# Two layers of an MLP behind attention on one core: the seven-product frames' half-units at 4, 2, 4, 4, one sum for two, and the conversion of w_out paced at two steps a pair

## The chip, the core and the metric

The kernel runs on one core of a Trainium2 chip. The metric is the device time in microseconds (us), the median of several runs. The engines are TensorE (PE, matrix products), VectorE (DVE), ScalarE (ACT), GpSimd (POOL) and SyncE (SP), which here only issues DMAs.

## What is computed

Attention over 4 batches, 8 heads, 576 tokens and 64 columns a head (half of the heads see the last 32 tokens, half see every 32nd), its output as 2304 tokens x 512, and then two MLPs of the same form:

```
def _moe_ref(x, w_in, w_out):        # x 2304x512, w_in 512x2048, w_out 2048x512
    h = x @ w_in
    r = np.maximum(h, 0.0)
    return (r * r) @ w_out           # called twice, with weights of its own each time
```

All is float32 to the caller. The kernel splits each operand of an MLP into a high part (fp32r) and the remainder, and takes three products: high x high, high x low, low x high.

## The kernel before

First attention and the first layer run mixed; then the first layer runs alone, beside the conversion of the second layer's weights, up to about 512 us; then comes one narrow block of 256 tokens of layer 2 (to about 545 us), and from there on the frames.

*Layer 1.* A list `steps` of pairs (block, f) is walked in order: mm1 of the next step (products into ps_h, then on ACT r, sq and gh, the high part of the squared relu, and on DVE gl, the remainder), then mm2 of this one (products of gh and gl into the four ps_y). After a block's last step ACT evicts ps_y (L1085) and the tile o is stored in y_dram (L1087): in the last two blocks from ACT's own queue, else from SP. Each step has 8 points (`point`), and at each a credit grows by PACES, 0.6 for w_out and 0.68 for w_in; a whole credit lets `conv2_by` issue one unit of converting layer 2's weights. A pair of w_out quarters is nine units: exponent and sign on raw and others (L263 on ACT), the high part of each quarter (L368, ACT), its remainder (rest2, DVE), the sums of quarters for the seven products (sums_1 to sums_3), and their high part (L420, ACT). Both quarters of a pair are stored in w_mem by one DMA of 1 MB (L378), the sums by another (L426); both tiles are used again by the next pair.

*The narrow block.* Eight steps; the products with w_out are at L1142. The last step's 12 stand inside the first frame.

*The frames.* Blocks of 512 tokens use a scheme of seven products for eight (as Strassen's). A frame works on one pair of hidden tiles: it makes the products with w_in of the next pair, in four visits (L1274), and puts the seven products with w_out of the current pair between them, as 14 half-units of three matmuls (L1301). All of a frame's visits write one PSUM tile of 512 columns, ps_m (in the first frame visits 3 and 4 have another). Visit 1 (12 matmuls) is copied away by ACT (u, L1354); visit 2 (6) overwrites the left half and is added to c11 by DVE (L1109); visit 3 (12) writes both halves, which DVE reads in three sums, u3, a22 and u4; visit 4 (12) writes both halves again, and DVE makes c from them (128x512). Behind each visit stands a gap with 3, 3, 5 and 3 half-units. Each engine runs its instructions in the order in which the code issues them. There are 31 frames with half-units, and the first one, with the 12 products of the narrow block in threes.

```
gaps = todo[:3], todo[3:6], todo[6:11], todo[11:]       # seven()
visit(k, q, ps, ("11", 0), ("s2", 1)); ... each(gaps[0])
visit(k, q, ps, ("12", 2)); add(c11, ps[:, :HT], c11); ... each(gaps[1])
visit(k, q, ps, ("s1", 3), ("s3", 4)); ... each(gaps[2])       # behind it the three sums
visit(k, q, ps, ("s4", 5), ("22", 6)); add(of["c"], ps, u); ... each(gaps[3])
```

Of the kernel before, what the change touches and what calls it, by code (L numbers as in the profile page):

```python
# [17 lines left out]
P = 128  # L18
# [6 lines left out]
NF = DFF // P  # L25
# [34 lines left out]
AT_V, AT_XN = P + 2 * P + 126, P + 2 * P + 126 + 5 * 260  # L60
OTHERS = AT_XN + 256 + 64

PACES = 0.6, 0.68
N_WARM = 8
ZEROS = (0, 0, 0, 0, 0, 2, 2, 2, 2, 4, 4, 4)

# [98 lines left out]
def r32(ap):  # L165
    return ap.bitcast(F32)
# [3 lines left out]
def tile_attention_then_two_mlps(  # L170
# [9 lines left out]
    nc = tc.nc  # L180
# [191 lines left out]
    def rest2(i):  # L372
        v = val[half1 + i].rearrange("p (h m) -> p h m", h=2)
        w = w_nat[i]
        nc.vector.tensor_tensor(out=w[:, :, 1], in0=v, in1=r32(w[:, :, 0]), op=ALU.subtract)
        done2.add(i)
        if i < NF and i % 2:
            nc.sync.dma_start(out=w_mem[i // 2][:, :4 * U], in_=r32(xall[:, units_at:units_at + 4 * U]))  # L378

    s_sum = {}  # L380

# [661 lines left out]
    def mm2(s, point):  # L1043

        k, f = steps[s]
        layer, j = blocks[k]
        t0, n = BLOCKS[layer][j]
        ne = tiles_of(k)
        ws = [ready(("out", layer, f + e)) for e in range(ne)]
        h, lo = gh.pop(s), gl.pop(s)  # L1050

        if f == 0:
            ys[k] = [ps_y.tile([P, 512], F32, tag=f"y{c}", name="ps_y") for c in range(KC)]
        end = f + ne == NF

        def narrow_at(s):
            return s < len(steps) and tiles_of(steps[s][0]) > 1

        todo = []
        for c, y in enumerate(ys[k]):  # L1060
            cols = slice(c * P, (c + 1) * P)
            for i, (a, gp) in enumerate(((0, h), (1, h), (0, lo))):
                for e, w in enumerate(ws):
                    g0 = e * n
                    todo.append((i, c, y[:, :n], w[:, a, cols], gp[:, g0:g0 + n]))
        if not end:

            todo.sort(key=lambda t: t[0] == 2)
        places = [-(-len(todo) * (i + 1) // 4) - 1 for i in range(3)]
        last = {t[1]: m for m, t in enumerate(todo)}  # L1070
        seen = set()
        for m, (i, c, y, lhsT, rhs) in enumerate(todo):
            product(
                y,
                lhsT=lhsT,
                rhs=rhs,
                start=f == 0 and c not in seen,
                stop=end and m == last[c],
                halves=m == len(todo) - 1 and rhs.shape[-1] == TB and narrow_at(s + 2),
            )  # L1080
            seen.add(c)
            one_small()
            if end and m == last[c]:
                t = tile_of("s" if c % 2 and j >= NB - 2 else "pt")[:, :n]
                nc.scalar.activation(out=t, in_=y, func=AF.Copy, scale=W_BACK)  # L1085
                queue = nc.scalar if j >= NB - 2 else nc.sync
                queue.dma_start(out=y_dram[:, c, t0:t0 + n], in_=t)  # L1087
            if m in places:
                point()

# [10 lines left out]
    def rest(hi, lo, src):  # L1101
        tt(lo, src, r32(hi), ALU.subtract)
# [5 lines left out]
    def add(dst, src, to, sign=1.0):  # L1108
        nc.vector.scalar_tensor_tensor(  # L1109
            out=dst, in0=src, scalar=sign * W_BACK, in1=to, op0=ALU.mult, op1=ALU.add  # L1110
        )
# [45 lines left out]
    def narrow(s, point):  # L1157
        q = steps[s][1] // 2
        ring_load(q)
        narrow_w(q + 1)  # L1160
        work = x_work.setdefault(NB + 1, x_works(NB + 1))
        if q + 1 < NF // 2:
            if q == 0:
                load_x(NB + 1, 0)
                load_x(NB + 1, 1)
            elif q > 1:
                all_of(work[q - 2])
            mm1(s + 1, point)
            point()
            for m, one in enumerate(narrow_products(s)):  # L1170
                one()
                if m % 3 == 2:
                    point()
            return
        while n_conv2[0] < len(conv2):
            conv2_by(1)
        all_of(work[-1])
        todo = narrow_products(s)
        frame([todo[3 * i:3 * i + 3] for i in range(4)], (NB + 1, 0), False)
        t0, n = BLOCKS[1][0]  # L1180
        for c, y in enumerate(ys[NB]):
            t = tile_of("pt")
            nc.scalar.activation(out=t, in_=y, func=AF.Copy, scale=W_BACK)
            nc.sync.dma_start(out=out[t0 + c * P:t0 + (c + 1) * P, :], in_=t)
# [128 lines left out]
    def frame(gaps, nxt, cur, copies=((), (), ()), end=False, x=((), (), ()), late=()):  # L1313

        k, q = nxt
        if not of:
            of["r"] = gpool.tile([P, TB], F32, tag="r", name="r", bufs=1)
            of["c"] = gpool.tile([P, TB], F32, tag="sq", name="c", bufs=1)
            shapes = {"bh": ("qk0", 4), "bl": ("qk1", 4), "ah": ("qk2", 3)}
            for t, (tag, n) in shapes.items():  # L1320
                of[t] = fpool.tile([P, n * HALF], F32R, tag=tag, name=t, bufs=1).rearrange(
                    "p (i n) -> p i n", i=n)
            for t, n in (("al", 2), ("al2", 1)):
                of[t] = gpool.tile([P, 3 * HALF], F32R, tag="gl", name=t, bufs=2)[
                    :, 48:48 + n * HALF].rearrange("p (i n) -> p i n", i=n)
        r, c = (of[t].rearrange("p (h n) -> p h n", h=2) for t in ("r", "c"))
        a11, a22, a21, a12 = r[:, 0], r[:, 1], c[:, 0], c[:, 1]
        ah, al, bh, bl = (of[t] for t in ("ah", "al", "bh", "bl"))
        sums_x, high_x, rest_x = x

        def positive(t, src):
            nc.scalar.activation(out=t, in_=src, func=AF.Relu)
            nc.scalar.activation(out=t, in_=t, func=AF.Square)

        if cur:
            s13, s24 = (
                gpool.tile([P, TB + P], F32, tag="gh", name="s", bufs=2)[:, :TB].rearrange(
                    "p (i n) -> p i n", i=2)
                for _ in range(2)
            )  # L1340
            high(ah[:, 2], a12)
            tt(s13[:, 0], a21, a22, ALU.add)
            tt(s13[:, 1], a11, a21, ALU.subtract)
            rest(ah[:, 2], of["al2"][:, 0], a12)
            tt(s24[:, 0], s13[:, 0], a11, ALU.subtract)
            tt(s24[:, 1], a12, s24[:, 0], ALU.subtract)
        each(copies[0])
        ps = ps_h.tile([P, TB], F32, tag="h", name="ps_m")
        visit(k, q, ps, ("11", 0), ("s2", 1))
        m, u = (vpool.tile([P, 512], F32, tag="val", name="u") for _ in range(2))  # L1350

        c11, u2 = m[:, :HT], m[:, HT:]
        u4, u3 = u[:, :HT], u[:, HT:]
        nc.scalar.activation(out=m, in_=ps, func=AF.Copy, scale=W_BACK)  # L1354
        tt(u2, c11, u2, ALU.add)
        each(copies[1])
        if cur:
            high(ah[:, 0:2], s13)
            high(bh[:, 2:4], s24)
        each(copies[2])  # L1360
        each(gaps[0])
        if end:
            first_sum()
        visit(k, q, ps, ("12", 2))
        add(c11, ps[:, :HT], c11)
        if cur:
            rest(bh[:, 2:4], bl[:, 2:4], s24)
            rest(ah[:, 0:2], al, s13)
        each(sums_x)
        if end:  # L1370
            each(high_x)
            each(rest_x)
        positive(a11, c11)
        high(bh[:, 0], a11)
        if not end:
            each(high_x)
        each(gaps[1])
        if nxt == pairs7[0]:
            ps = ps_a.tile([P, TB], F32, tag="a", name="ps_m")
        visit(k, q, ps, ("s1", 3), ("s3", 4))  # L1380
        add(u3, ps[:, HT:], u2)
        add(a22, ps[:, :HT], u3)
        add(u4, ps[:, :HT], u2)
        positive(a22, a22)
        high(bh[:, 1], a22)
        rest(bh[:, 0], bl[:, 0], a11)
        if not end:
            each(rest_x)
        each(gaps[2])
        each(late)  # L1390
        rest(bh[:, 1], bl[:, 1], a22)
        visit(k, q, ps, ("s4", 5), ("22", 6))
        add(of["c"], ps, u)
        squares(of["c"])
        each(gaps[3])
# [4 lines left out]
    def first_sum():  # L1400
        acc["p1"] = tile_of("pt")
        nc.scalar.activation(out=acc["p1"], in_=banks["11"], func=AF.Copy, scale=W_BACK)
# [105 lines left out]
    def seven():  # L1508
        copies, sums = None, []
        for n, (k, q) in enumerate(pairs7[:-1]):  # L1510
            todo = [one for name in ORDER for one in n_unit(k, q, name)]
            gaps = todo[:3], todo[3:6], todo[6:11], todo[11:]
            end = q == NF // 2 - 1 or n + 2 == len(pairs7)
            more = k < last7
            x = [[], [], []]
# [131 lines left out]
```

## Time and profile before

| | |
|---|---|
| median of 3 runs | 867.05 us (866.18 to 868.54) |
| the profiled execution | 866.58 us |
| its span, from the first to the last instruction | 864.8 us |
| mean granted clock of TensorE, share of the higher level | 0.999 |
| busy: PE / DVE / ACT | 851.5 / 683.0 / 526.1 us |
| DMA over the span | 155.21 MB, 179 GB/s |

A matmul is pipelined: its row begins when it starts, and its end is modelled, so that two neighbours overlap in the rows. How fast TensorE works is read from the distance between starts. An idle time in brackets counts from the modelled end of the row before.

### The profile page before, as it was taken

What the parts mean: (1) busy time and instruction counts of PE and PEld (TensorE: products, weight loads), DVE (VectorE), ACT (ScalarE), POOL (GpSimd) and SP (SyncE); (2) the same over time, 40 slices, a digit from 0 to 9 for tenths busy, and PEclk for the clock granted to TensorE, in tenths of its full rate; (3) what the DMA queues carried; (4) which work ended last, traced back from release to release, by engine and by line L of the source; (5) the groups of instructions that cost most, each with busy time, mean ns of one, the idle gap of its engine ahead of it and who ended that gap; (6) DMA issues with size and microseconds to landing.
All of it is one profiled execution on the core that took longest, in us unless ns stands there. A gap on an engine that the chain in (4) does not pass through costs nothing. (4 is left out here: it accounts for less than half of the span.)

```text
span 864.8 us, 16060 instructions
## 1 busy us (share of the span) xinstructions
PE 851.5 (98%) x5719; PEld 771.6 (89%) x5719; DVE 683.0 (79%) x1742; ACT 526.1 (61%) x1216; POOL 17.7 (2%) x15
## 2 busy tenths in 40 slices
PE   9899999999999999999999999999999999999997
PEld 8778888888788888899788899899999999999997
DVE  5899895489776777477889977678888889888877
ACT  6987775467665665375767774555554564556442
POOL 0610000000000000000000000000000000000000
PEclk9999999999999999999999999999999999999999
DMA  8965721222222221167988486376668667766764
GB/s 257 343 216 154 240 65 43 89 78 73 72 82 97 75 61 53 70 219 293 338 324 265 146 281 232 131 221 207 195 186 281 193 187 240 245 188 194 231 186 130
DMA packets 81247, 155.21 MB, mean 179 GB/s; under 512 B 7440, under 2 KB 36240, under 8 KB 78096
## 3 DMA queue, kind: packets, MB, share of 16 engines
q1 hardware_dynamic: 80016, 152.62, 54.2%
q10 hardware_dynamic: 1152, 1.57, 0.5%
q8 instruction: 45, 0.74, 0.3%
q14 instruction: 34, 0.28, 0.1%
HBM read 127.95 MB, written 26.21 MB: 178 GB/s over the span
## 5 line engine op out<-in xcount | busy, mean ns | idle before, releaser
L971 PE MATMUL ps_h<-xall,w 128*128 128x512 f32 (+1 forms) x1153 | 247.3, 358 | 0.0
L971 PEld LDWEIGHTS ps_h<-xall,w 128*128 128x128 f32 x1153 | 185.1, 188 | 25.9
L971 PE MATMUL ps_y<-gh,w 128*128 128x512 f32 (+1 forms) x640 | 156.8, 375 | 2.3 <-ACT gh L1020 1.6
L971 PEld LDWEIGHTS ps_y<-gh,w 128*128 128x128 f32 x640 | 107.7, 188 | 20.5 <-ACT gh L1020 2.2
L1274 PE MATMUL ps_m<-xall,s 128*128 128x256 f32 x768 | 104.8, 279 | 0.6 <-DVE u L1109 0.6
L1274 PEld LDWEIGHTS ps_m<-xall,s 128*128 128x128 f32 x768 | 95.5, 188 | 1.8 <-DVE u L1109 1.0
L1301 PE MATMUL ps_y<-w,bh 128*128 128x256 f32 x496 | 91.8, 278 | 0.0
L1014 ACT ACTIVATE r<-ps_h 128x512 f32<-128x512 f32 x80 | 47.4, 593 | 62.1 <-PE ps_h L971 52.8
L971 PE MATMUL ps_y<-gl,w 128*128 128x512 f32 (+1 forms) x324 | 83.9, 370 | 0.5 <-DVE gl L1025 0.5
L1274 PE MATMUL ps_m<-xall,w 128*128 128x256 f32 x576 | 83.4, 281 | 0.0
L1301 PEld LDWEIGHTS ps_y<-w,bh 128*128 128x128 f32 x496 | 75.3, 188 | 0.0
L1274 PEld LDWEIGHTS ps_m<-xall,w 128*128 128x128 f32 x576 | 74.3, 188 | 0.4 <-ACT u L1354 0.4
L1301 PE MATMUL ps_y<-w,ah 128*128 128x256 f32 x372 | 70.0, 278 | 0.0
L1025 DVE TENSOR_TENSOR gl<-sq,gh 128x512 fp32r<-128x512 f32 x80 | 55.2, 690 | 17.6 <-ACT gh L1020 13.2
L1301 PE MATMUL ps_y<-w,bl 128*128 128x256 f32 x248 | 68.8, 277 | 0.0
L1023 DVE TENSOR_TENSOR sq<-r 128x512 f32<-128x512 f32 x38 | 26.3, 692 | 49.2 <-ACT r L1014 49.2
L971 PEld LDWEIGHTS ps_y<-gl,w 128*128 128x128 f32 x324 | 55.7, 188 | 10.4 <-DVE gl L1025 1.2
L1109 DVE SCALAR_TENSOR_TENSOR u<-ps_m,u 128x256 f32<-128x256 f32 x96 | 40.4, 421 | 26.4 <-PE ps_m L1274 26.3
L1099 ACT ACTIVATE ah<-c 128x256 fp32r<-128x256 f32 x33 | 13.7, 418 | 71.3 <-DVE c L1283 71.1
L1301 PEld LDWEIGHTS ps_y<-w,ah 128*128 128x128 f32 x372 | 56.7, 189 | 0.0
L676 ACT ACTIVATE s<-s,m 96x128 f32<-96x128 f32 (+2 forms) x88 | 34.3, 390 | 34.3 <-DVE m L560 33.7
L1301 PE MATMUL ps_y<-w,al 128*128 128x256 f32 x186 | 51.6, 277 | 0.0
(121 smaller groups left out, 1505.7 us busy)
## 6 DMA issues: line engine op xcount, KB each, us to landing
w<-w_mem SPq DMA_DIRECT2D x221, 256.0 KB, 2.8
raw<-moe_w_in_d SPq DMA_DIRECT2D x32, 512.0 KB, 6.1
w_mem<-xall SPq DMA_DIRECT2D x16, 1024.0 KB, 5.3
raw<-moe_w_out_d SPq DMA_DIRECT2D x24, 512.0 KB, 5.1
xall<-w_mem SPq DMA_DIRECT2D x8, 1024.0 KB, 5.1
qk<-loc_qk_d SPq DMA_DIRECT2D x12, 416.0 KB, 3.1
out_d<-o SPq DMA_DIRECT2D x17, 256.0 KB, 2.6
others<-moe_w_out_d SPq DMA_DIRECT2D x8, 512.0 KB, 7.1
```

The lines of the kernel that those rows point to most:

```text
L676: nc.scalar.activation(out=blk, in_=blk, func=AF.Exp, scale=-1.0, bias=m[:nq, j:j + 1], accum_out=dens[i][:nq, j:j + 1],)
L971: nc.tensor.matmul(y[:, c:c + w], lhsT=lhsT, rhs=rhs[:, c:c + w], start=start and c == 0, stop=stop and c + w == n,)
L1014: nc.scalar.activation(out=r, in_=ps, func=AF.Relu, scale=W_BACK)
L1023: nc.vector.tensor_tensor(out=sq, in0=r, in1=r, op=ALU.mult)
L1025: nc.vector.tensor_tensor(out=lo, in0=sq, in1=r32(h), op=ALU.subtract)
L1099: nc.scalar.activation(out=hi, in_=src, func=AF.Copy)
L1109: nc.vector.scalar_tensor_tensor(out=dst, in0=src, scalar=sign * W_BACK, in1=to, op0=ALU.mult, op1=ALU.add)
L1274: nc.tensor.matmul(ps[:, half * HT:(half + 1) * HT], lhsT=w[:, j * P:(j + 1) * P], rhs=x[:, j], start=half == 0 and j == 0 and m == 0, sto ...
L1301: nc.tensor.matmul(banks[name][:, t * HALF:(t + 1) * HALF], lhsT=g[:, rows], rhs=w, start=first and t == 0 and m == 0, stop=end and t == 1 ...
```

## The change

Five edits. (1) `gaps` holds 4, 2, 4 and 4 half-units; in the first frame the 12 products of the narrow block stand 4, 2, 4 and 2. (2) u3 and u4, two additions of u2 to the halves of visit 3's tile, become one instruction of 512 columns, ahead of a22. (3) PACES for w_out is 0.56. (4) Each quarter of w_out is stored by itself as soon as its remainder is made, in two DMAs of 512 KB. (5) The stores of y_dram of the last two blocks go from SP as the others do; and in the frame that ends a block the remainder of ah stands ahead of visit 2 and its sum instead of behind.

```diff
-PACES = 0.6, 0.68
+PACES = 0.56, 0.68
...
-        if i < NF and i % 2:
-            nc.sync.dma_start(out=w_mem[i // 2][:, :4 * U], in_=r32(xall[:, units_at:units_at + 4 * U]))
+        if i < NF:
+            a = i % 2 * 2 * U
+            nc.sync.dma_start(
+                out=w_mem[i // 2][:, a:a + 2 * U],
+                in_=r32(xall[:, units_at + a:units_at + a + 2 * U]),
+            )
...
-                queue = nc.scalar if j >= NB - 2 else nc.sync
-                queue.dma_start(out=y_dram[:, c, t0:t0 + n], in_=t)
+                nc.sync.dma_start(out=y_dram[:, c, t0:t0 + n], in_=t)
...
-        frame([todo[3 * i:3 * i + 3] for i in range(4)], (NB + 1, 0), False)
+        frame((todo[:4], todo[4:6], todo[6:10], todo[10:]), (NB + 1, 0), False)
...
         if end:
             first_sum()
+            rest(ah[:, 0:2], al, s13)
         visit(k, q, ps, ("12", 2))
         add(c11, ps[:, :HT], c11)
         if cur:
             rest(bh[:, 2:4], bl[:, 2:4], s24)
+        if cur and not end:
             rest(ah[:, 0:2], al, s13)
...
-        add(u3, ps[:, HT:], u2)
+        add(
+            u.rearrange("p (h n) -> p h n", h=2),
+            ps.rearrange("p (h n) -> p h n", h=2),
+            u2.unsqueeze(1).to_broadcast([P, 2, HT]),
+        )
         add(a22, ps[:, :HT], u3)
-        add(u4, ps[:, :HT], u2)
...
-            gaps = todo[:3], todo[3:6], todo[6:11], todo[11:]
+            gaps = todo[:4], todo[4:6], todo[6:10], todo[10:]
```

TensorE from the second half-unit behind visit 1 to visit 3 of a frame, before. Visits are L1274, half-units L1301; bh, bl, ah and al are parts of the squared relu (a number behind al tells two of them apart).

```order
L1301 MATMUL ps_y<-w,bh 128x256 x2
L1301 MATMUL ps_y<-w,bl 128x256
L1301 MATMUL ps_y<-w,ah 128x256 x2
L1301 MATMUL ps_y<-w,al_5986 128x256
L1274 MATMUL ps_m<-xall,w 128x256 x6
L1301 MATMUL ps_y<-w,ah 128x256 x2
L1301 MATMUL ps_y<-w,al_5986 128x256
L1301 MATMUL ps_y<-w,bh 128x256 x2
L1301 MATMUL ps_y<-w,bl 128x256
L1301 MATMUL ps_y<-w,bh 128x256 x2
L1301 MATMUL ps_y<-w,bl 128x256
L1274 MATMUL ps_m<-xall,s 128x256 x12
```

The same place after (the lines are three further on):

```order
L1304 MATMUL ps_y<-w,bh 128x256 x2
L1304 MATMUL ps_y<-w,bl 128x256
L1304 MATMUL ps_y<-w,ah 128x256 x2
L1304 MATMUL ps_y<-w,al_5994 128x256
L1304 MATMUL ps_y<-w,ah 128x256 x2
L1304 MATMUL ps_y<-w,al_5994 128x256
L1277 MATMUL ps_m<-xall,w 128x256 x6
L1304 MATMUL ps_y<-w,bh 128x256 x2
L1304 MATMUL ps_y<-w,bl 128x256
L1304 MATMUL ps_y<-w,bh 128x256 x2
L1304 MATMUL ps_y<-w,bl 128x256
L1277 MATMUL ps_m<-xall,s 128x256 x12
```

One half-unit (two matmuls and one) has moved from behind visit 2 to in front of it; visit 3 begins three matmuls sooner behind visit 2.

DVE in the same frame, before, from visit 2's sum (the first row) to c:

```order
L1109 SCALAR_TENSOR_TENSOR u<-ps_m,u 128x256
L386 TENSOR_TENSOR bl<-s,bh 128x512
L386 TENSOR_TENSOR al<-s,ah 128x512
L1109 SCALAR_TENSOR_TENSOR u<-ps_m,u 128x256
L1109 SCALAR_TENSOR_TENSOR r<-ps_m,u 128x256
L1109 SCALAR_TENSOR_TENSOR u<-ps_m,u 128x256
L386 TENSOR_TENSOR bl<-r,bh 128x256 x2
L1109 SCALAR_TENSOR_TENSOR c<-ps_m,u 128x512
```

And after:

```order
L1112 SCALAR_TENSOR_TENSOR u<-ps_m,u 128x256
L390 TENSOR_TENSOR bl<-s,bh 128x512
L390 TENSOR_TENSOR al<-s,ah 128x512
L1112 SCALAR_TENSOR_TENSOR u<-ps_m,u 128x512
L1112 SCALAR_TENSOR_TENSOR r<-ps_m,u 128x256
L390 TENSOR_TENSOR bl<-r,bh 128x256 x2
L1112 SCALAR_TENSOR_TENSOR c<-ps_m,u 128x512
```

The sum of 512 columns stands where the first of 256 stood, and the last of the three is gone.

ACT at the end of the fourth layer-1 block, before: r, sq and gh belong to a step, o to the evictions, the rest to the conversion.

```order
L368 ACTIVATE xall<-val 128x2x256
L1014 ACTIVATE r<-ps_h 128x512
L1019 ACTIVATE sq<-r 128x512
L1020 ACTIVATE gh<-sq 128x512
L1085 ACTIVATE o<-ps_y 128x256
L1087 DMA y_dram<-o 128x256
L368 ACTIVATE xall<-val 128x2x256
L1085 ACTIVATE o<-ps_y 128x256
L1087 DMA y_dram<-o 128x256
L1085 ACTIVATE o<-ps_y 128x256
L1087 DMA y_dram<-o 128x256
L1085 ACTIVATE o<-ps_y 128x256
```

And after, from a step's r to the next conversion:

```order
L1018 ACTIVATE r<-ps_h 128x512
L1023 ACTIVATE sq<-r 128x512
L1024 ACTIVATE gh<-sq 128x512
L1089 ACTIVATE o<-ps_y 128x256 x4
L368 ACTIVATE xall<-val 128x2x256 x2
L1018 ACTIVATE r<-ps_h 128x512
L1023 ACTIVATE sq<-r 128x512
L1024 ACTIVATE gh<-sq 128x512
L424 ACTIVATE xall<-raw 128x4x256
```

The four evictions stand together, without the issues of their stores, and both L368 copies of a pair follow them.

## Rows read from the trace of the kernel before

**Rows 1.** the page, busy us (share of the span) and instructions of each engine
```profile
PE 851.5 (98%) x5719; PEld 771.6 (89%) x5719; DVE 683.0 (79%) x1742; ACT 526.1 (61%) x1216; POOL 17.7 (2%) x15
```

**Rows 2.** windows by stage: length, then busy PE, PEld, DVE, ACT, POOL; PEclk, DMA
```profile
366.00:422.00 56.00, 53.90 (x419) 50.59 (x419) 41.54 (x75) 35.79 (x60) 0.00 (x0) 1.00 0.72 262
512.00:545.00 33.00, 32.70 (x216) 29.67 (x215) 24.64 (x42) 18.39 (x31) 0.00 (x0) 1.00 0.68 241
...
553.00:854.00 301.00, 300.99 (x2594) 300.32 (x2594) 253.41 (x552) 160.68 (x347) 0.00 (x0) 1.00 0.67 210
```

**Rows 3.** timeline of TensorE, one frame: start, us, engine, line, operation, count [idle <-releaser]
```profile
561.86 0.85 PE L1274 MATMUL ps_m<-xall,w 128*128 128x256 f32 x6
...
564.25 0.87 PE L1274 MATMUL ps_m<-xall,w 128*128 128x256 f32 x6
...
566.02 1.54 PE L1274 MATMUL ps_m<-xall,s 128*128 128x256 f32 x12
...
569.10 0.87 PE L1274 MATMUL ps_m<-xall,s 128*128 128x256 f32 x6
...
571.58 0.40 PE L1274 MATMUL ps_m<-xall,w 128*128 128x256 f32 x2
```

**Rows 4.** timeline of DVE in the same frame
```profile
565.16 0.43 DVE L1109 SCALAR_TENSOR_TENSOR u<-ps_m,u 128x256 f32<-128x256 f32 x1 [0.48 <-PE ps_m L1274]
...
567.60 0.42 DVE L1109 SCALAR_TENSOR_TENSOR u<-ps_m,u 128x256 f32<-128x256 f32 x1 [0.81 <-PE ps_m L1274]
...
568.40 0.41 DVE L1109 SCALAR_TENSOR_TENSOR u<-ps_m,u 128x256 f32<-128x256 f32 x1
...
570.72 0.69 DVE L1109 SCALAR_TENSOR_TENSOR c<-ps_m,u 128x512 f32<-128x512 f32 x1 [0.43 <-PE ps_m L1274]
```

**Rows 5.** timeline of TensorE, end of a layer-1 block
```profile
407.78 2.90 PE L971 MATMUL ps_h<-xall,w 128*128 128x512 f32 x13
411.60 0.74 PE L971 MATMUL ps_y<-gh,w 128*128 128x256 f32 x4 [0.91 <-ACT gh L1020]
...
413.22 0.62 PE L971 MATMUL ps_y<-gh,w 128*128 128x256 f32 x4
...
415.27 2.90 PE L971 MATMUL ps_h<-xall,w 128*128 128x512 f32 x12
418.01 0.62 PE L971 MATMUL ps_y<-gh,w 128*128 128x512 f32 x2
...
421.32 0.86 PE L971 MATMUL ps_y<-gl,w 128*128 128x512 f32 x3
```

**Rows 6.** timeline of ACT there; ACTq is its queue of DMA issues
```profile
408.12 1.06 ACT L420 ACTIVATE xall<-others 128x1024 fp32r<-128x1024 f32 x1 [2.36 <-DMA w_mem<-xall]
...
417.82 0.34 ACTq L1087 DMA_DIRECT2D y_dram<-o  x1
```

**Rows 7.** timeline of TensorE, narrow block's start and the first frame
```profile
511.31 1.10 PE L971 MATMUL ps_h<-xall,w 128*128 128x256 f32 x8
512.71 2.11 PE L1142 MATMUL ps_y<-xall,gh 128*128 128x512 f32 x8 [0.30 <-ACT gh L1020]
514.66 0.96 PE L1142 MATMUL ps_y<-xall,gl 128*128 128x512 f32 x4
...
544.70 0.84 PE L1142 MATMUL ps_y<-xall,gh 128*128 128x512 f32 x3
...
547.04 1.58 PE L1274 MATMUL ps_m<-xall,s 128*128 128x256 f32 x12
548.46 0.61 PE L1142 MATMUL ps_y<-xall,gh 128*128 128x512 f32 x2
548.91 0.39 PE L1142 MATMUL ps_y<-xall,gl 128*128 128x512 f32 x1
549.93 0.97 PE L1274 MATMUL ps_m<-xall,s 128*128 128x256 f32 x6 [0.63 <-DVE u L1109]
```

**Rows 8.** the page, DMA issues: KB each, us from issue to landing
```profile
w_mem<-xall SPq DMA_DIRECT2D x16, 1024.0 KB, 5.3
```

More of the change, by code (lines that the diff above doesn't have):

```diff
@@ L1352, in frame @@
         c11, u2 = m[:, :HT], m[:, HT:]
-        u4, u3 = u[:, :HT], u[:, HT:]
+        u3 = u[:, HT:]
         nc.scalar.activation(out=m, in_=ps, func=AF.Copy, scale=W_BACK)
```

## Prediction

> **What bounds the kernel now.** First the page: TensorE (PE) is busy 98% of a span of 864.8 us [rows 1]. A change can therefore gain in two ways only: where PE stands still, or where its matmuls start closer together. Next the busy times by stage, where the granted clock is 1.00, the higher of TensorE's two levels (2.4 GHz), in every one [rows 2]. From 553 to 854 us, the second layer's seven-product frames, PE is busy 300.99 of 301.00 us: nothing is missing there, DVE's 253 us fit beside it, and whatever is removed from DVE or ACT is worth nothing until PE itself moves. From 366 to 422 us PE is busy 53.90 of 56.00 us: there it waits. Third, TensorE's rows in time order. A row's start is a fact and its end is modelled, so I count from start to start.
>
> **One frame.** The frame of [rows 3] starts its visits at 561.86, 564.25, 566.02 and 569.10 us and the next frame at 571.58: 9.72 us. Its 84 matmuls are all 256 columns wide, but the spacing has two values: 21 matmuls in 2.39 us (0.1138 each), 15 in 1.77 (0.118), 27 in 3.08 (0.114), 21 in 2.48 (0.118). I call 0.1138 fast and 0.1182 slow. The spacing changes at each step from half-units to a visit. Had all 84 been fast, the frame would last 9.56 us, so the slow part costs 0.16. The order of the frame shows what stands between two such steps: 21, 15, 27, 21 matmuls, all odd. After the change it is 24, 12, 24, 24, all even.
>
> All visits of a frame write one PSUM tile, so each also waits until what the last one left there is read. From [rows 3] and [rows 4] I take two distances. A visit's last matmul begins one spacing ahead of the next row, for the second visit 564.25 + 5 x 0.118 = 564.84; DVE's read begins at 565.16, that is 0.32 later. The tightest visit of the frame, at 571.58, comes 0.17 after the read it waits for (570.72 + 0.69 = 571.41). So a visit can begin no sooner than last matmul + 0.32 + DVE's work + 0.17. After the third visit DVE's work is three sums, from 567.60 to 568.81; 0.17 more gives 568.98, and the visit came at 569.10: 0.12 to spare.
>
> **The change, part by part.**
>
> *Gaps 4, 2, 4, 4 and the joint sum, 31 frames.* PE's instructions are the same in number. Behind visit 1 a half-unit more (3 matmuls, 0.34 us) can only relax visit 2, which ACT's copy u releases and which does not wait now. Behind visit 2 there are 6 matmuls in place of 9. With the last matmul at L, the third visit would come at L + 7 x 0.1138 = L + 0.80; the limit is L + 0.32 + 0.43 + 0.17 = L + 0.92. It waits 0.12. Behind visit 3, 12 in place of 15: nominal L + 13 x 0.1138 = L + 1.48; DVE now does one 128x512 sum and one 128x256 sum in place of three of 256. An addition of 512 from PSUM lasts 0.69 in this frame (the c row), one of 256 0.41 to 0.43 [rows 4], so L + 0.32 + 0.69 + 0.03 + 0.42 + 0.17 = L + 1.63, a wait of 0.15. The removed addition thus gives DVE 0.07 us back where the gap was cut by 0.34, which uses up the 0.12 to spare. Behind visit 4, 12 in place of 9: the next frame gains 0.34 over a margin that is now nil.
>
> What the two waits cost depends on the spacing between them. Fast everywhere, the frame is 53 spacings of 0.1138 (6.03) + 0.92 + 1.25 + 1.63 = 9.83 us, where 1.25 is the third visit's 11 spacings up to its last matmul: +0.11 a frame, +3.4 over 31. With the two values taking turns as now it is 9.95: +0.23, +7.1 in all. Slow everywhere, 10.10: +0.38, +11.8. Fast everywhere with no wait, 9.56: -0.16, -5.0. These are the ends; I take +3.4. My reason is the oddness above: layer 1's steps hold 24 products, an even count, and run at one spacing (12 of 512 columns from 415.27 to 418.01 [rows 5] are 0.228 each, twice 0.114), while the stretches that change pace are the odd ones. It is a pattern in rows, not a known cause.
>
> On the spacing the Trainium skill has a rule, in "TensorE: Matmul & The Clock Gate", Part 1, section "Wait — 56ns, not 53.3ns?": at full clock start-to-start is N / 2.4 GHz plus about 2.5 ns whatever comes before, so by that page an estimate of 109 ns for 256 columns. The trace disagrees on the value (113.8 and 118) and shows two of them. By that rule the order of visits and half-units is worth nothing and only waits count; this is the first rival below.
>
> *w_out conversions at 0.56 a point.* Nine units make a pair of w_out quarters and a step has 8 points, so a pair now takes 9 / 0.56 = 16 points, two whole steps; before it took 15 and its place wandered against the steps. I put three stalls of PE down to this. (A) ACT waits 2.36 us for a store of w_mem to release its tile, up to 408.12 [rows 6], its relu and gh come late, and PE waits for gh: from 407.78 to 413.22 it takes 5.44 us for 12 products of 512 columns (2.74; the last is in two pieces) and 6 of 256 (0.68): 2.0 us [rows 5]. (B) At the end of a block ACT's four evictions o stand between conversions and four issues of stores on ACT's own queue, 0.34 each [rows 6]; 8 products starting at 418.01 take 3.31 us where 8 x 0.228 = 1.82 are due: 1.5 us [rows 5]. (C) From 511.31 to 514.66, 8 products of 256 and 8 of 512 take 3.35 where 0.91 + 1.82 are due, with a wait for gh between: 0.6 us [rows 7]. After the change the order has r, sq and gh ahead of the conversions' copies in each step, and the four evictions in a row: I take A, B and C as gone, 4.1 us. If what they wait for only moves, they stay: 0.
>
> *Store in two halves.* Eight 1 MB stores become sixteen of 512 KB; the first half no longer waits for the second quarter. A 1 MB store lands in 5.3 us at the median [rows 8]. In a pair's 10.9 us (two steps) even two full landings back to back would end in time, which is why I take this as no cost; it is costed together with A above.
> The Trainium skill speaks against it, in "DMA: Bandwidth & Descriptors", section "Bandwidth": transfers should be batched to 1 MiB or more. By that page's single-transfer fit (2 us plus the bytes at 436 GB/s) two halves are an estimate of 6.4 us in all against 4.4 for one; no run here shows a 512 KB store to w_mem yet, the rows have 5.3 for the 1 MB one.
>
> *Eight y stores from ACT to SP.* ACT loses eight issues, in B 4 x 0.34 = 1.4 us of its time. On SP they wait for ACT's evictions, and the next loads of weights stand behind them; those are loaded several us ahead of use, so nothing on PE is late by the 1.5 us over which four evictions last (four times about 0.4, an addition of that width on DVE being 0.42).
>
> *The first frame* (545 to 553 us), whose half-units are 512 wide: 4, 2, 4, 2. Visit 2 there waits for ACT's copy: from 544.70 to 547.04 six products and the visit take 2.34 where 6 x 0.228 + 6 x 0.116 = 2.06 are due, 0.28; visit 4 waits for DVE's sums, the product at 548.91 taking 1.02 for 0.23, 0.8 [rows 7]. One product of 0.228 more ahead of each removes the first and leaves 0.5 to 0.6 of the second: -0.5. Visit 3 has a tile of its own and doesn't wait.
>
> *The earlier rest in the four block ends* puts 0.69 of DVE ahead of the addition that visit 3 waits for. With 6 matmuls of cover gone this may cost up to 0.5 in four frames; DVE does it while visit 2 runs, so I take 0, with +2 as the other end.
>
> *Conversions end one step later* (8 pairs, 1 point each), which puts them into the narrow stage, where DVE is busy 24.64 of 33.00 us [rows 2]: covered but for +0.2, a small reserve with no row of its own.
>
> Sum: -2.0 - 1.5 - 0.6 - 0.5 + 0.2 = -4.4, and +3.4 from the frames: -1.0. The profiled execution took 866.58 us (span 864.8 and 1.8 around it); 865.6 is 866.05 on the median, which lies 0.47 above it.
>
> **The rivals.**
> 1. *The spacing keeps taking turns* whatever the count. For it: nothing but parity speaks of why it turns. Then the frames cost 7.1: 866.58 - 4.4 + 7.1 + 0.47 = 869.8.
> 2. *Slow everywhere: the slower side.* Even counts keep the state that a frame starts in, and if a wait leaves PE in the slow one, nothing turns it back. For it: after a stall either spacing follows, 0.114 from 415.27 us [rows 5] and 12 matmuls in 1.42, 0.118, from 547.04 [rows 7]. Against: the whole step at 415.27 stays fast. The place is every frame from 553 us on; it decides as soon as a frame lasts longer than 9.86 us (4.4 / 31 = 0.14 more). +11.8 - 4.4: 874.5.
> 3. *The waits don't bite and all is fast*: if DVE begins closer to the visit's end or a visit needs less than 0.17 behind DVE. -5.0 - 4.4: 857.7. Against it are two distances read at more than one visit.
> 4. *The change doesn't do what it says*: the stalls A to C move with the stores instead of vanishing, and only the frames' +3.4 stays: 870.5.
>
> **How the numbers follow.** The forecast has 0.46, alone 863.6 to 868.5; rivals 1 to 4 have 0.17, 0.15, 0.13 and 0.09. A measurement of this kernel can tell 0.3%, 2.6 us: faster is below 864.45, slower above 869.65. Faster: 0.12 of the forecast and rival 3, 0.25. Slower: rival 2, about half of rival 1 and two thirds of rival 4, and 0.01 of the forecast, 0.31. Same: 0.44. The range, 860.0 to 874.0, leaves out most of rival 3 and over half of rival 2.
>
> **What would show it.** In TensorE's rows a frame of 9.83 us, all rows of two matmuls at one spacing, visit 3 released by DVE's c11 about 0.1 late and visit 4 by the sum a22 about 0.15 late, visit 2 and the next frame without a wait; no wait for gh near 411, 419 and 512 us. A frame of 9.95 or more with 0.118 in it shows rival 1 or 2; 9.6 shows rival 3. I am wrong if PE still waits for ACT over 1 us in layer 1, or if the visits show no wait.

## The result, and the profile after

The changed kernel takes 871.88 us (median of 6 runs, 871.08 to 872.95) against 867.31 before (866.18 to 868.68): a ratio of 1.0051, 95% interval 1.0038 to 1.0064, slower by 4.6 us. The forecast was 866.1; the time lies in its range and on the side that had 31%. Its profiled execution took 871.08 us, span 869.3 against 864.8. One execution of a later kernel (the parts put together, below) took 1044.72 us at a mean granted clock of 0.753 and stands in no comparison.

Where the 4.5 us of span come from is read by matching the same matmul in both traces (their order is the same up to the frames):

| stretch | before | after | difference | forecast |
|---|---|---|---|---|
| from the start to the 1500th matmul ahead of the first frame | 275.4 | 273.9 | -1.4 | not touched by the change |
| stalls A and B (384 to 430 us of before) | 45.3 | 41.8 | -3.5 | -3.5 |
| from there into the narrow block, with C | 87.0 | 90.4 | +3.4 | -0.6, and +0.2 in reserve |
| the first frame | 8.85 | 8.24 | -0.6 | -0.5 |
| the frames to the last one | 292.7 | 299.6 | +6.85 | +3.4 |

(Between 275 and 384 us and in the rest of the narrow block nothing differs by over 0.1; the end is 0.2 shorter.) The first line differs by as much between traces of kernels that are the same up to there (273.9 here, 275.6 and 276.0 in two runs below): this execution happened to be ahead in the attention. The other lines add up to 6.1. The last line holds 30 frames from start to start; the 31st stands in the end.

By stage, columns as in [rows 2]: layer 1 now has no gap (PE 56.00 of 56.00 us), but there is one at 507 us, and behind it a stretch at a granted clock of 0.50, the lower of the two levels:

```profile
366.00:422.00 56.00, 56.00 (x430) 53.48 (x429) 42.31 (x76) 39.89 (x67) 0.00 (x0) 1.00 0.81 294
507.00:509.60 2.60, 0.45 (x4) 0.27 (x4) 2.46 (x6) 2.05 (x4) 0.00 (x0) 1.00 0.97 367
511.00:514.00 3.00, 3.00 (x10) 2.43 (x8) 2.40 (x5) 1.48 (x2) 0.00 (x0) 0.50 1.03 420
514.00:516.00 2.00, 2.00 (x19) 2.00 (x19) 1.56 (x3) 0.00 (x0) 0.00 (x0) 0.99 0.78 198
```

TensorE there: the 8 products of the narrow block's second step wait 2.15 us for a load and then take 2.68 us in place of 1.82, the next 5 rows (4 products' worth of 512 columns) 1.71 in place of 0.91.

```profile
504.46 2.99 PE L975 MATMUL ps_h<-xall,w 128*128 128x256 f32 x24
509.61 2.89 PE L1145 MATMUL ps_y<-xall,gh 128*128 128x512 f32 x8 [2.15 <-DMA xall<-w_mem]
512.29 1.89 PE L1145 MATMUL ps_y<-xall,gl 128*128 128x512 f32 x5
514.00 2.25 PE L975 MATMUL ps_h<-xall,w 128*128 128x256 f32 x18
```

SP's queue of the changed kernel shows why. The load of these weights (the second xall<-w_mem) is issued at 502.41, behind four stores of y, which wait for ACT's evictions, the first of them from 486.4 to 498.83 us:

```profile
485.90 0.50 SPq L1124 DMA_DIRECT2D xall<-w_mem  x1
498.83 2.35 SPq L1090 DMA_DIRECT2D y_dram<-o  x4
501.27 0.39 SPq L225 DMA_DIRECT2D raw<-moe_w_in_d  x1
...
502.41 0.47 SPq L1124 DMA_DIRECT2D xall<-w_mem  x1
```

The evictions on ACT, four from 498.22 to 500.82 us:

```profile
498.22 0.58 ACT L1089 ACTIVATE o<-ps_y 128x512 f32<-128x512 f32 x1
...
499.26 1.56 ACT L1089 ACTIVATE o<-ps_y 128x512 f32<-128x512 f32 x3
```

Before, the same two loads:

```profile
490.86 0.50 SPq L1121 DMA_DIRECT2D xall<-w_mem  x1
...
500.36 0.43 SPq L1121 DMA_DIRECT2D xall<-w_mem  x1
```

There the second one was issued 12.35 us ahead of the products that need it (512.71, [rows 7]). Now these products could come at 507.3, 4.9 us behind the issue, and the load lands at 509.47, 7.1 us behind it: it is late.

The visits of two frames of the changed kernel, which answer to [rows 3]:

```profile
560.13 0.85 PE L1277 MATMUL ps_m<-xall,w 128*128 128x256 f32 x6
...
562.86 0.87 PE L1277 MATMUL ps_m<-xall,w 128*128 128x256 f32 x6
...
564.28 1.62 PE L1277 MATMUL ps_m<-xall,s 128*128 128x256 f32 x12
...
567.15 0.95 PE L1277 MATMUL ps_m<-xall,s 128*128 128x256 f32 x6
...
568.62 0.39 PE L1304 MATMUL ps_y<-w,ah 128*128 128x256 f32 x2
...
569.98 0.87 PE L1277 MATMUL ps_m<-xall,w 128*128 128x256 f32 x6
...
572.81 0.85 PE L1277 MATMUL ps_m<-xall,w 128*128 128x256 f32 x6
```

From 560.13 to 562.86 24 matmuls take 2.73 us (0.114), the next 12 1.42 (0.118), the next 24 2.87, the next 24 2.83, and from 569.98 to 572.81 the same 24 that took 2.73 take 2.83 (0.118): both spacings are there, though all counts are even. Behind the wait at visit 4 the spacing is fast (12 half-unit matmuls from 568.62 to 569.98 take 1.36, 0.113), as it was ahead of it: this step did not change it. The waits are those of the forecast. DVE in that frame, answering to [rows 4]:

```profile
563.78 0.43 DVE L1112 SCALAR_TENSOR_TENSOR u<-ps_m,u 128x256 f32<-128x256 f32 x1 [1.02 <-PE ps_m L1277]
...
565.94 0.69 DVE L1112 SCALAR_TENSOR_TENSOR u<-ps_m,u 128x512 f32<-128x512 f32 x1 [0.54 <-PE ps_m L1277]
566.67 0.42 DVE L1112 SCALAR_TENSOR_TENSOR r<-ps_m,u 128x256 f32<-128x256 f32 x1
...
568.82 0.69 DVE L1112 SCALAR_TENSOR_TENSOR c<-ps_m,u 128x512 f32<-128x512 f32 x1
```

Visit 2's last matmul starts at 562.86 + 5 x 0.118 = 563.45, DVE reads at 563.78 (0.33 later) and the limit is 563.78 + 0.43 + 0.17 = 564.38: between the first matmul of visit 3 (564.28) and its second (564.48), which is where TensorE stands. Visit 3's sums end at 567.09; 0.17 more is 567.26, and visit 4's second matmul comes at 567.37, 0.15 later than at the fast spacing.

The first frame lasts from 541.74 to 549.98, 8.24 us, and its visit 4 still waits for DVE:

```profile
541.74 0.87 PE L1277 MATMUL ps_m<-xall,w 128*128 128x256 f32 x6
...
548.05 0.95 PE L1277 MATMUL ps_m<-xall,s 128*128 128x256 f32 x6 [0.32 <-DVE r L1112]
...
549.98 0.87 PE L1277 MATMUL ps_m<-xall,w 128*128 128x256 f32 x6
```

### The profile page after: what moved, and what is told of

The parts are those of the page before. It is cut to its first block, busy times and chain, and to the rows that moved or that the text cites. A ratio compares the mean times of both kernels' runs of the same rounds, so it can differ in the third digit from the quotient of the medians.

```text
span 869.3 us, 16027 instructions
## 1 busy us (share of the span) xinstructions
PE 857.3 (99%) x5719; PEld 776.0 (89%) x5719; DVE 680.7 (78%) x1709; ACT 527.4 (61%) x1217; POOL 17.1 (2%) x15
## 4 chain that ended last, share of the span: by engine, by line
PE 91%; DVE 4%; DMA 2%; ACT 2%; issue 0%; SPq 0%; DVEq 0%; ACTq 0%
PE ps_h L975 24%; PE ps_y L975 22%; PE ps_m L1277 18%; PE ps_y L1304 16%; PE ps_y L1145 2%; PE ps_x L708 2%; PE ps_s L632 2%; PE ps_pt L764 2%; PE ps_s L534 1%; PE ps_o L780 1%; DMA xall<-w_mem 1%; DMA raw<-moe_w_in_d 1%; PE ps_y L1478 0%; DMA y_dram<-o 0%; DMA qk<-loc_qk_d 0%; DVE val L268 0%
## 5 line engine op out<-in xcount | busy, mean ns | idle before, releaser
L1277 PE MATMUL ps_m<-xall,s 128*128 128x256 f32 x768 | 111.0, 287 | 0.6 <-DVE r L1112 0.3
L1112 DVE SCALAR_TENSOR_TENSOR u<-ps_m,u 128x256 f32<-128x256 f32 x64 | 35.7, 558 | 34.8 <-PE ps_m L1277 34.8
```

The source lines that it names most:

```text
L1112: nc.vector.scalar_tensor_tensor(out=dst, in0=src, scalar=sign * W_BACK, in1=to, op0=ALU.mult, op1=ALU.add)
L1277: nc.tensor.matmul(ps[:, half * HT:(half + 1) * HT], lhsT=w[:, j * P:(j + 1) * P], rhs=x[:, j], start=half == 0 and j == 0 and m == 0, sto ...
```

## The experiments

All of the twelve that were timed stand beside runs of the kernel before on the same chip (866.8 to 867.2 us).

**The half-units back at 3, 3, 5, 3.**

```diff
-            gaps = todo[:4], todo[4:6], todo[6:10], todo[10:]
+            gaps = todo[:3], todo[3:6], todo[6:11], todo[11:]
```

> The changed kernel with 3, 3, 5, 3 half-units again in the 31 frames; all else as changed (the first frame keeps 4, 2, 4, 2). Theory (the waits at visits 3 and 4 cost what they showed, the spacing of matmuls does not depend on the count of half-units): the frames are 9.72 us again, both waits gone, 7.0 us less than the changed kernel's 871.9: 864.9. Rival (the frames are slower for another reason, the joint sum or the stores): no change, 871.9.

Measured: 864.50 us, ratio 0.9973 (0.9964 to 0.9983). The gaps cost 7.4 us. Matmuls that TensorE gets done from 553 to 840 us (the x behind PE busy), before:

```profile
553.00:840.00 287.00, 286.99 (x2473) 286.32 (x2473) 242.92 (x528) 154.11 (x333) 0.00 (x0) 1.00 0.68 212
```

changed:

```profile
553.00:840.00 287.00, 286.71 (x2416) 283.50 (x2415) 235.88 (x486) 149.70 (x324) 0.00 (x0) 1.00 0.66 207
```

changed, with 3, 3, 5, 3:

```profile
553.00:840.00 287.00, 287.00 (x2479) 286.91 (x2479) 241.53 (x499) 154.59 (x334) 0.00 (x0) 1.00 0.68 212
```

63 matmuls more than the changed kernel, at 287 / 2479 = 0.116 us each 7.3 us.

**4, 2, 4, 4 alone, in the kernel before** (three sums, all else as before).

> The kernel before with 4, 2, 4, 4 half-units in the 31 frames alone; three separate sums, all else as before. Theory (waits, spacing taking turns as before): visit 3 waits 0.12 and visit 4 0.22 of a us a frame, 10.5 for 31, less the 1.3 that stand there now: 876.5. Rival (the even counts keep all matmuls at the fast spacing): 5.7 less of slow spacing, 871.

Measured: 878.12 us, ratio 1.0128 (1.0114 to 1.0141): +10.9, where the waits alone were expected to give 10.5 - 1.3 = 9.2. The rival with the fast spacing is out by 7 us. Matmuls in the same stretch:

```profile
553.00:840.00 287.00, 284.89 (x2379) 280.35 (x2377) 235.82 (x510) 148.16 (x320) 0.00 (x0) 1.00 0.65 205
```

**The joint sum alone, in the kernel before.**

> The kernel before with the joint sum of u3 and u4 alone. Theory (with 3, 3, 5, 3 DVE's three sums end 0.12 us before visit 4 needs them; sooner is worth only the 0.8 us of small waits at visit 4 in a few frames): 866.4, or no change that can be told. Rival (the joint sum of 512 itself delays a22 and with it TensorE): slower than before, 868 or more.

Measured: 866.05 us, ratio 0.9991 (0.9982 to 1.0000): worth 0.8 us by the medians, 0 to 1.6 by the interval, and 0.4 in the frames of its trace. It pays mostly where visit 4 waits (with it and the rest of the change, 4, 2, 4, 4 costs 7.4 in place of 10.9).

**The y stores on ACT's queue again, in the changed kernel.**

```diff
-                nc.sync.dma_start(out=y_dram[:, c, t0:t0 + n], in_=t)
+                queue = nc.scalar if j >= NB - 2 else nc.sync
+                queue.dma_start(out=y_dram[:, c, t0:t0 + n], in_=t)
```

> The changed kernel with the y stores of the last two layer-1 blocks on ACT's queue again; all else as changed. Theory (on SP these stores wait for ACT's evictions and hold up the load of the narrow block's second weights, so that TensorE waits 2.3 us at 507 us and then runs at the lower clock for some 3 us): the load is issued before 499 us, the wait and the low clock go, 3.9 us less, less some 0.6 for ACT's issues: 868 to 868.6. Rival (the load is late because of the conversions that end later, or the split stores): the wait stays, 871.9.

Measured: 869.97 us, ratio 1.0038 (1.0025 to 1.0051): 1.9 us less by the medians, not 3.3 to 3.9; in the traces the stretch from the 600th matmul ahead of the first frame to this frame is 2.7 shorter. The wait for the load is gone, and a wait for gh of 0.97 stands in its place:

```profile
506.07 2.99 PE L975 MATMUL ps_h<-xall,w 128*128 128x256 f32 x24
510.03 2.12 PE L1146 MATMUL ps_y<-xall,gh 128*128 128x512 f32 x8 [0.97 <-ACT gh L1024]
```

ACT shows its reason: the issue of the fourth y store stands until 506.64, and r, sq and gh of the step stand behind it. In the trace this issue waits for the semaphore of the first of the four stores, which lands at 506.57.

```profile
503.37 0.60 ACT L1089 ACTIVATE o<-ps_y 128x512 f32<-128x512 f32 x1 [0.40 <-ACT o L1089]
506.64 0.33 ACTq L1091 DMA_DIRECT2D y_dram<-o  x1
507.01 1.16 ACT L368 ACTIVATE w<-val 128x512 fp32r<-128x512 f32 x2 [3.05 <-DMA y_dram<-o]
```

The kernel before has the same wait, and its C comes from it: the fourth issue stands until 509.75, and r, sq and gh of the step follow.

```profile
510.18 0.67 ACT L263 ACTIVATE raw<-raw 128x512 f32<-128x512 f32 x1 [1.85 <-DMA y_dram<-o]
```

In the changed kernel with the stores on ACT the clock stays at 1.00 after its wait:

```profile
510.00:514.00 4.00, 3.97 (x23) 3.49 (x24) 3.96 (x6) 3.65 (x6) 0.00 (x0) 1.00 0.56 217
```

**Both at once.**

> Both of the above at once: 3, 3, 5, 3 half-units in the frames and the y stores on ACT. Theory (two causes that add): 864.9 - 3.6 = 861.3, from 860.5 to 862.5. If either cause is not one, the time of the other alone: 865 or 868.

Measured: 861.68 us, ratio 0.9945 (0.9931 to 0.9958), within what was expected: 10.2 us less than the changed kernel, where the two alone give 7.4 and 1.9. In its trace the frames are 7.6 shorter and the stretch ahead of them 2.6. The two causes add.

**The load ahead of the y stores, which stay on SP** (and 3, 3, 5, 3).

```diff
             mm1(s + 1, point)
+            if s + 1 == first_2:
+                narrow_w(1)
...
-        narrow_w(q + 1)
+        if q:
+            narrow_w(q + 1)
```

> The changed kernel with 3, 3, 5, 3 half-units, the y stores on SP, and the load of the narrow block's second weights issued ahead of the last block's y stores instead of behind them. Theory (the wait at 507 us and the low clock behind it come from the place of this load in SP's queue): 2.5 us of waiting and 1.6 of low clock go: 864.5 - 4.1 = 860.4, and below the 861.7 with the stores on ACT, since ACT then has no issue to wait with. Rival (the load is slow because of the traffic beside it, wherever it stands): the wait stays or moves to the next step of the narrow block: 862 to 864.5.

Measured: 861.42 us, ratio 0.9937 (0.9924 to 0.9949): 3.1 us less than with the load behind the stores, where 4.1 were expected, and level with the stores on ACT. SP issues both loads from 486.81 on:

```profile
486.81 4.00 SPq L1124 DMA_DIRECT2D xall<-w_mem  x2
499.74 2.35 SPq L1090 DMA_DIRECT2D y_dram<-o  x4
...
506.05 0.38 SPq L1124 DMA_DIRECT2D xall<-w_mem  x1
```

The products start at 508.20 without a wait, and the clock does not fall; a wait of 0.46 for the third load stands one step later (at 514.29), so that a part of the rival holds too:

```profile
508.20 1.98 PE L1145 MATMUL ps_y<-xall,gh 128*128 128x512 f32 x8
...
514.29 1.88 PE L1145 MATMUL ps_y<-xall,gh 128*128 128x512 f32 x7 [0.46 <-DMA xall<-w_mem]
```

**The pace of w_out back at 0.6** (with 3, 3, 5, 3 and the y stores on ACT).

> The kernel with 3, 3, 5, 3 and the y stores on ACT (861.7 us), with w_out's pace at 0.6 again; the stores in halves stay. Theory (the pace removed the waits near 411 and 419 us): they are back, 3.5 us: 865.2. Rival (the halves or the stores removed them): 861.7.

Measured: 860.78 us, ratio 0.9932 (0.9920 to 0.9945). With the halves in place the pace is not what removes A and B: they don't come back. This is the lowest median of all runs, 6.1 us below the kernel before, though its interval overlaps those of the next ones.

**One store of 1 MB again** (with 3, 3, 5, 3, the y stores on ACT and the pace at 0.56).

> The kernel with 3, 3, 5, 3 and the y stores on ACT (861.7 us), with w_out's quarters in one store of 1 MB again; the pace stays at 0.56. Theory (the halves are worth nothing beside the pace): 861.7. Rival (the earlier first half is what keeps ACT from waiting for its tile): a wait of 1 to 2 us near 411 us is back, 863 to 864.

Measured: 862.46 us, ratio 0.9956 (0.9943 to 0.9969): 0.8 more than with the halves, within the intervals, and no wait near 411 us. With the pace at 0.56 the halves are not needed there.

**The halves alone, and the pace alone, each in the kernel before.**

> The kernel before with w_out's quarters stored in two halves, and nothing else. Theory (the first half's early store is enough by itself to remove the waits near 400 to 420 us): 867.0 - 3.5 = 863.5. Rival (it takes halves and pace, or another part of the change): 867.0. A page of the Trainium skill has it that halves cost more transfer time; if that decided, 867.5 or more.

> The kernel before with w_out's pace at 0.56, and nothing else. Theory of the prediction (the pace by itself removes the waits near 400 to 420 us): 867.0 - 3.5 = 863.5, perhaps 0.8 more for a wait near 509 us that stood in the run with one store: 864.3. Rival (the pace alone is worth nothing): 867.

Measured: the halves 862.33 us, ratio 0.9946 (0.9934 to 0.9959); the pace 863.37, 0.9962 (0.9949 to 0.9974). Each removes A and B by itself. From 396 to 422 us, the kernel before, the halves alone, the pace alone:

```profile
396.00:422.00 26.00, 23.90 (x166) 21.03 (x165) 18.56 (x33) 15.93 (x27) 0.00 (x0) 1.00 0.80 298
```

```profile
396.00:422.00 26.00, 26.00 (x181) 23.98 (x180) 21.88 (x39) 18.64 (x33) 0.00 (x0) 1.00 0.92 338
```

```profile
396.00:422.00 26.00, 26.00 (x181) 24.06 (x180) 18.24 (x33) 16.97 (x29) 0.00 (x0) 1.00 0.80 293
```

TensorE is busy 23.90, 26.00 and 26.00 of 26 us, and the stretch of A and B takes 41.8 us with either, as with both. The two don't add: both shorten ACT's waits for stores of w_mem, which come to 21.3 us in all before, 11.6 with the halves alone and 10.5 with the pace alone. B hangs on such a wait too. Before, it ends just ahead of the r, sq, gh and evictions of that block end:

```profile
415.07 0.63 ACT L368 ACTIVATE xall<-val 128x512 fp32r<-128x512 f32 x1 [2.95 <-DMA w_mem<-xall]
```

**The parts put together** (3, 3, 5, 3, pace 0.6, halves, the load ahead of the y stores), and the same with the first frame's products at 3, 3, 3, 3.

> What the runs point to: 3, 3, 5, 3 half-units in the frames, the joint sum, the first frame at 4, 2, 4, 2, w_out's pace at 0.6, stores in halves, the y stores on SP with the load of the narrow block's second weights ahead of them. Theory (the place of the load and the pace are separate): a little below the 860.8 of the pace at 0.6 with the y stores on ACT, by its last wait of 0.4 near 509 us: 860.4. Rival (at 0.6 SP's queue or ACT is late elsewhere): 861.4 to 864.

> The kernel that the runs point to, with the first frame's 12 products at 3, 3, 3, 3 again. Theory of the prediction (4, 2, 4, 2 saves 0.5 us there): 0.5 to 0.6 us slower than the one beside it. Rival: the same.

Measured: 861.90 us, ratio 0.9940 (0.9926 to 0.9954), where 860.4 was expected, so the order of the loads adds nothing to the 860.78 with the y stores on ACT; and 863.13, 0.9956 (0.9942 to 0.9969). The first frame's 4, 2, 4, 2 is worth 1.2 by the medians, whose intervals overlap; in the traces it takes 8.80 us with 3, 3, 3, 3 against 8.24 in the changed kernel, so 0.56.

**A PSUM tile for each visit.** The theory of the forecast was that odd counts of matmuls change the spacing. The rivals are the step from half-units to a visit, and the short wait there. Visits 3 and 4 get a tile in the same way; the rest of the edit fits the sums to the shared banks.

```diff
+                shared = {"s1t1": "s2t2", "s3t3": "a22t4", "s4b22": "12"}.get(name)
...
+        ps = ps_a.tile([P, TB], F32, tag="a", name="ps_m")
         visit(k, q, ps, ("12", 2))
...
```

> The kernel with the pace at 0.6 and the y stores on ACT, with 4, 2, 4, 4 half-units, and each of a frame's four visits in a PSUM tile of its own; to free the banks three of the seven products are added into the banks of three others, so that part of the output is not the reference's. The visits keep their semaphores, but none waits for the visit just before it. Theory (the waits at visits 3 and 4 are the price of 4, 2, 4, 4, and the spacing changes at each step from half-units to a visit whatever the count): 9.72 to 9.75 us a frame, 0.118 in about 40% of it. Rival of the prediction (an even count leaves the spacing as it is): one spacing throughout, 9.56 or 9.93. Second rival (it is the short wait at a visit that changes the spacing): one spacing throughout, here and in the run with 3, 3, 5, 3.

> The same with 3, 3, 5, 3 half-units and a tile for each visit. Theory: 9.72 us a frame, both spacings, as with one tile. Rival of the prediction (odd counts change the spacing): also 9.72. Second rival (short waits change it): one spacing throughout, 9.56 or 9.93.

Measured (one run each, which also carries waits of about 1.3 us at each new block, since the shared banks must be read first): 867.79 and 870.47 us, beside 866.42 for the kernel before. What counts is a frame within a block, 4, 2, 4, 4:

```profile
567.26 0.85 PE L1278 MATMUL ps_m<-xall,w 128*128 128x256 f32 x6
...
570.00 0.87 PE L1278 MATMUL ps_m<-xall,w 128*128 128x256 f32 x6
...
571.42 1.54 PE L1278 MATMUL ps_m<-xall,s 128*128 128x256 f32 x12
...
574.15 0.87 PE L1278 MATMUL ps_m<-xall,s 128*128 128x256 f32 x6
...
576.98 0.85 PE L1278 MATMUL ps_m<-xall,w 128*128 128x256 f32 x6
```

No row waits, the frame lasts 9.72 us, and its 24, 12, 24 and 24 matmuls take 2.74, 1.42, 2.73 and 2.83: 0.114, 0.118, 0.114, 0.118. With either split the frames within a block last 9.72 or 9.77 but for one in each run: without the waits 4, 2, 4, 4 costs nothing. So the spacing changes without odd counts and without waits: in these two traces it does so at 240 of the 242 steps from half-units to a visit that don't wait. Where visits wait it is less regular: in the changed kernel all 61 steps to visits 1 and 2 change the spacing, but 35 of the 61 to visits 3 and 4, which wait, leave it as it was. With 4, 2, 4, 4 alone in the kernel before, 13 of 30 steps to visit 1 leave it too, without a wait. Why it changes there, and not at the step from a visit to half-units, no run tells.

## Why the prediction was wrong

*The frames: the spacing failed, the waits were right.* The forecast took +3.4, "fast everywhere", and called the oddness "a pattern in rows, not a known cause". It wasn't the cause. The step that failed is the 0.16 us a frame, 5.0 in all, that the forecast took off for the slow spacing: with even counts 1104 of the changed kernel's 2580 matmuls in the frames stand in stretches at the slow spacing, and 1065 of 2583 before (a stretch runs from one visit to the next and is put down by its median distance). Rival 1, the spacing that keeps taking turns, had 7.1 for this term; measured are 6.85 in the traces and 7.4 in the runs. The price came, though the turns are not as regular as rival 1 has them. The waits themselves were sized as measured: 0.12 and 0.15 a frame were forecast, and the matmuls at visits 3 and 4 of the changed kernel exceed the fast spacing by 0.10 and 0.165 a frame. The Trainium skill's rule that was weighed there ("TensorE: Matmul & The Clock Gate", Part 1, "Wait — 56ns, not 53.3ns?") led to the right conclusion here, that only waits count, though not to the right values: the traces have 113.4 and 118 ns where it gives an estimate of 109.

*The y stores on SP: "nothing on PE is late" failed.* The forecast named the loads that stand behind these stores, but set "several us ahead of use", which it took from no row, against 1.5 us of evictions, which it worked out from a width of 256. The last block's evictions are 128x512 and last 2.6 us in all, and SP stands at the first store until they begin: the load of the narrow block's second weights is issued 4.9 us ahead of its use and takes 7.1. With C this term is +3.4 in place of -0.6: a wait of 2.3 us from start to start, and 1.6 us at the lower clock. The runs with the stores on ACT and with the load ahead of them both take it away. That a wait can bring the lower clock with it, no row of before showed. C itself did go, though not by the order of the conversions: it hung on the issue of the fourth y store on ACT, and came back, as 0.97, when the stores did.

*A and B: the sum was right, the cause half.* -3.5 as forecast, but put down to the pace. Either the pace or the halves alone do it, and the halves, which the forecast took as no cost and gave no gain of their own, are worth 4.6 us by themselves (3.5 of them at A and B in the trace). The Trainium skill spoke against them ("DMA: Bandwidth & Descriptors", "Bandwidth": batch to 1 MiB). The page after shows what the rule and the runs each say, KB and us to landing:

```profile
w_mem<-xall SPq DMA_DIRECT2D x16, 512.0 KB, 3.5
w_mem<-xall SPq DMA_DIRECT2D x8, 1024.0 KB, 5.2
```

Two halves take 7.0 us in all against 5.2 for one store of 1 MB (here those of the sums, which stayed whole), as the rule has it; but the first half leaves one quarter earlier, and a half lands sooner than a whole. B went with A in the runs that left all y stores on ACT, so that the issues between the evictions, which the forecast blamed, were not its cause.

*The first frame, the earlier rest and the later conversions* came as forecast: -0.6, and nothing that the traces show.

*The chances.* Rival 1's price came (17%), beside a loss at 507 us that no rival had. That the time still lies in the range is luck: the range was drawn for other rivals and has no room of its own for that loss. The forecast's own case had 46% on a pattern seen at two kinds of places.

## What to carry to other kernels

A matmul engine that never waits can be slowed by moving its work alone: before half-units are moved from behind one read to behind another, the time from the last matmul to the end of that read (here 0.32 + DVE's work + 0.17 us) is set against the matmuls that are left there, at every visit. An instruction that waits is moved to another queue only after the entries that will stand behind it have been read, and for each the time from issue to landing is set against the time to its use. A pattern of timing is not counted as a gain until a run has broken it.

## What the runs showed of the hardware

- 256-column matmuls start 113.4 or 118 ns apart at a granted clock of 1.00. In the two runs with a tile for each visit the value changes at 240 of 242 steps from half-units to a visit that don't wait, after 12 to 27 matmuls; behind a wait either value follows.
- After a stand of 2.3 us TensorE of the changed kernel ran on at a granted clock of 1.00 for about a microsecond and then at 0.50 for 3.4 us (510.6 to 514.0 us). After one of 1.1 us in the run with the stores on ACT the clock stayed at 1.00, but so it did after one of 2.3 us in the run with 4, 2, 4, 4 and a tile for each visit, so the length of a stand does not tell alone (its row, and the window from 859 to 862 us):

```profile
859.01 0.50 PE L1481 MATMUL ps_y<-w,ah 128*128 128x256 f32 x2 [2.14 <-DVE o L1113]
859.00:862.00 3.00, 2.99 (x25) 2.99 (x26) 1.26 (x2) 0.00 (x0) 0.00 (x0) 1.00 0.37 126
```

- The fourth y store on ACT's queue was issued only when the first of the four had landed, whose semaphore it waits for, and held ACT for 3.05 us.
